# Divisors on four column quarters, and key sums two blocks at a time, in a fused hash attention and gated feed-forward kernel

## The chip, the cores and the metric

The kernel runs on one core of a Trainium2 chip. The core has a matrix engine (TensorE, PE in the profile), a vector engine (VectorE, DVE), a scalar engine (ScalarE, ACT), a general engine (GpSimd, POOL) and queues that issue transfers (SyncE, SP, has the one that matters here). Each works through its own instructions in order and waits on semaphores for the others. SBUF is the memory the engines work in, 128 partitions wide; PSUM holds what TensorE writes. The metric is the device time of one execution in microseconds (us).

## The reference

Two blocks, one after the other. Attention has 4 batches of 8 heads, 768 tokens, head dimension 64. Queries and keys are projected on 6 random directions, the signs of the projections make a bucket number, and a query sees only the keys of its own bucket:

```python
mask = q_bucket[:, :, :, None] == k_bucket[:, :, None, :]
scores = np.where(mask, scale * np.matmul(q, k.transpose(0, 1, 3, 2)), -1000000000.0)
attn = np.exp(scores - np.max(scores, axis=-1, keepdims=True))
attn = attn / (np.sum(attn, axis=-1, keepdims=True) + 1e-09)
attn_out = np.matmul(attn, v)
```

The result, laid out as x with 3072 rows (tokens) and 512 columns, goes through a feed-forward with 2048 inner columns; the result is float32:

```python
h = x @ w_in
sp = np.maximum(h, 0.0) + np.log1p(np.exp(-np.abs(h)))
out = (h * erf(sp)) @ w_out
```

## The kernel before

**Pairs, halves and groups.** The 32 heads are worked in 16 pairs, two heads (`ab` = 0, 1) side by side in the two halves of the partitions. The 768 queries of a pair are two halves of 384 (HS), so there are 32 halves `h` (NH). The 768 keys of a half are six blocks of 128, in two groups `n` of three (GC). A score (`score`, L521) puts 128 keys on the partitions and 384 queries of both heads on the columns: for each head a bfloat16 product of the bucket bits, which adds a penalty for a foreign bucket, and a float32 product of k and q, into one PSUM tile `st`, of which there are three. ScalarE takes the exponential of it into SBUF (`exponential`, L535): block e, 128 keys by 2 x 384 queries, with one more column of ones. There are nine blocks of e, used in a ring.

**Sums and products of e.** The divisor of the softmax is the sum of e over all 768 keys. VectorE first adds the six blocks of a half into one, five additions of 128x768 (`sum_keys`, L547). TensorE then adds over the partitions by a product with ones (`divisor`, L592): per head one product with 64 columns of ones, the heads on partitions 0 to 63 and 64 to 127 of `z_ps`, so each sum stands there 64 times. Meanwhile TensorE has formed e times v (`weigh`, L561, tile `av`), two heads on the two column halves of the array. ScalarE copies both out (`keep_divisor` L604 to `z`, `leave` L613 to `x`).

**The reciprocals go through DRAM.** For a pair, SP stores one row of z for each head (`spread`, L633), loads the 1536 sums back as 128 partitions by 12 (`gather`, L637), VectorE adds a small number and takes the reciprocal (`invert`, L645 and L648), SP stores them (`ungather`, L653) and loads each head's row into 64 partitions (`widen`, L662). VectorE multiplies x by them (`normalise`, L670), and SP stores the pair's x (`send`, L676). In the same SP queue stand the loads of later pairs (`start_pair`, L342 and L347).

**Beside it.** For each next pair TensorE projects q and k (`hash_bits`, L358), ScalarE takes the signs, VectorE spreads them (L382, L392). ScalarE squares q and k into x_sum, a tile that the feed-forward uses later, only to sum the squares (`measure`, L579). 32 pieces of w_in and w_out, which arrive in float64, are converted by ScalarE and VectorE (L445 to L507), and VectorE forms sums of w_in (`presum_weights`, L691) and of the first block of x (`presum_x`, L326). A last part, `late`, does the divisor of the last half and the last pair's chain at the start of the feed-forward.

**The order of the work** is fixed by a planner, `arrange`. Every step is an `op` with an engine, a cost in us, a rank, the steps that it must follow, and a delay until others may see it; the planner lets each engine take the open step that can start first, lowest rank first. TensorE's own order is written out: for half h the scores of groups 2h+1 and 2h+2, the bits of the next pair after every second half, the divisor of half h-1, then both groups of `weigh` of half h. Its costs there are 0.82 us for a score, 2.02 for a group of `weigh`, 0.72 for a divisor. Tiles are followed for semaphores by the parts of them that are read and written.

**The feed-forward** (from about 340 us) forms both products with seven block products instead of eight, on the sums made before; TensorE, VectorE and ScalarE work through it in 24 steps. The change does not touch it.

Of the kernel before, what the change touches and what calls it, by code (L numbers as in the profile page):

```python
# [54 lines left out]
F32 = mybir.dt.float32  # L55
BF16 = mybir.dt.bfloat16
# [3 lines left out]
ALU = mybir.AluOpType  # L60
# [3 lines left out]
P = 128  # L64
# [16 lines left out]
class Op:  # L81
# [20 lines left out]
    exponential=(3.56, 5.29),  # L102
# [91 lines left out]
def kernel(  # L194
# [11 lines left out]
    nc = tc.nc  # L206
    B, H, S, D = v.shape
    NBIT = proj2.shape[1] // 2
    NPAIR = B * H // 2
# [3 lines left out]
    HS = S // 2  # L213
    JP = NPAIR // B
    GC = NC // 2
# [18 lines left out]
    ones = const.tile([P, D], F32, name="ones")  # L234
# [7 lines left out]
    blocks = []  # L242
# [16 lines left out]
    for c, (end, factor) in enumerate(  # L259
# [9 lines left out]
            out=steps[:, c : c + 1],  # L269
            in0=row,  # L270
# [12 lines left out]
    def bank(name):  # L283
        return misc.tile([P, 512], F32, name=name, tag="bank")
# [116 lines left out]
    def attention():  # L401
        NS = NPAIR * 4
        with (
# [17 lines left out]
            raws = {}  # L421

            def fetch_weights(n):
                if n >= len(pieces):
# [102 lines left out]
                        )  # L527

            def block(n, c):
                return etiles[(n * GC + c) % len(etiles)]  # L530

            def exponential(n, c):
                st = pairs[n // 4].pop(("st", n, c))
# [2 lines left out]
                    out=e[:, :, 0:HS], in_=st[:, :, 0:HS], func=AF.Exp, scale=scale  # L536
                )

            def sum_keys(n, c):
                d = pairs[n // 4]  # L540
                key = "sum", n // 2 % 2
                if n % 2 == 0 and c == 1:
                    d[key] = sums.tile([P, 2, HS], F32, name="sum", tag="sum")
                    before = block(n, 0)[:, :, 0:HS]
                else:
                    before = d[key]
                nc.vector.tensor_tensor(  # L547
                    out=d[key], in0=before, in1=block(n, c)[:, :, 0:HS], op=ALU.add
                )

            def weigh(n):
                half, g = n // 2 % 2, n % 2
# [23 lines left out]
            def measure(i, n, half):  # L576

                cols = slice(half * HS, (half + 1) * HS)
                nc.scalar.activation(  # L579
                    out=x_sum[:, 0, :, :].rearrange("p k t -> p (k t)")[:, 0:HS],  # L580
                    in_=pairs[i]["qk"[n]][:, cols],
                    func=AF.Square,
                    accum_out=stats[:, n, i, half : half + 1],
                )

            def divisor(h):

                i, half = divmod(h, 2)
                d = pairs[i]
                z = d["z_ps"] = bank("z_ps")[:, 0:HS]  # L590
                for ab in range(2):
                    nc.tensor.matmul(  # L592
                        out=z[ab * D : ab * D + D, :],
                        lhsT=ones,
                        rhs=d["sum", half][:, ab, :],
                        start=True,
                        stop=True,
                    )
# [28 lines left out]
            def spread(i):  # L627

                d = pairs[i]
                zd = d["zd"] = dram.tile([2, S], F32, name="zd", tag="zd")  # L630
                d["zc"] = small.tile([P, 2 * S // P], F32, name="zc", tag="zc")
                for ab in range(2):
                    nc.sync.dma_start(out=zd[ab : ab + 1, :], in_=d["z"][ab * D : ab * D + 1, :])  # L633

            def gather(i):
                d = pairs[i]
                nc.sync.dma_start(  # L637
                    out=d["zc"],
                    in_=d.pop("zd")[:, :].rearrange("a (p c) -> (a p) c", c=2 * S // P),
                )  # L640

            def invert(i):
# [6 lines left out]

            def ungather(i):  # L650
                d = pairs[i]
                rd = d["rd"] = dram.tile([2, S], F32, name="rd", tag="rd")
                nc.sync.dma_start(  # L653
                    out=rd[:, :].rearrange("a (p c) -> (a p) c", c=2 * S // P), in_=d["zc"]
                )
# [88 lines left out]
            for what, n in order:  # L744
                if what == "score":
                    i = n // 4
                    after = tuple(("weigh_bits", i, ab) for ab in range(2)) + (("copy_bits", i),)
                    for c in range(GC):
                        free = (slots[-3],) if len(slots) >= 3 else ()
                        pe(score, (n, c), 0.82, after + free)  # L750
                        slots.append(("exponential", n, c))
                elif what == "bits":
                    pe(bits_of, (n,), 1.34, (("start_pair", n), slots[-3]))
                    slots.append(("sign_of", n))
                elif what == "divisor":
                    last = 2 * n + 1
                    pe(divisor, (n,), 0.72, (("sum_keys", last, GC - 1), ("keep_divisor", n - 1)))
                else:
                    h = n // 2
                    after = (("exponential", n, GC - 1),)  # L760
                    if n % 2 == 0:
                        after += (("leave", h - 1), ("leave_plain", (h - 1) // 2))
                    pe(weigh, (n,), 2.02, after)
            for n in range(NS):
                for c in range(GC):
                    op(
                        exponential,
                        (n, c),
                        "ACT",
                        0.735,  # L770
                        (0, n, c),
                        (
                            ("score", n, c),
                            ("weigh", n - 3),
                            ("sum_keys", n - 3, c),
                            ("sum_keys", n - 3, max(c, 1)),
                        ),
                    )
                    if n % 2 or c:
                        after = (("exponential", n, c), ("exponential", n, 0))  # L780
                        after += (("sum_keys", n, c - 1), ("sum_keys", n - 1, GC - 1))
                        if n % 2 == 0:
                            after += (("divisor", n // 2 - 2),)
                        op(sum_keys, (n, c), "DVE", 0.92, (1, n, c), after)
            for h in range(NH - 1):
                i = h // 2
                op(
                    keep_divisor,
                    (h,),
                    "ACT",  # L790
                    0.48,
                    (0, 2 * h, -1),
                    (("divisor", h), ("send", i - 1) if i == NPAIR - 1 else ("widen", i - 1)),
                )
# [5 lines left out]
            for i in range(NPAIR):  # L800
# [32 lines left out]
                        )  # L833
                if i == NPAIR - 1:
                    continue
                op(spread, (i,), "SP", 0.8, (0, n, 0), (("keep_divisor", 2 * i + 1),), late=3.0)
# [788 lines left out]
```

## Time and profile before

| | |
|---|---|
| median of 13 runs | 937.61 us (935.67 to 939.91) |
| the profiled execution | 935.43 us, its span 933.5 us |
| TensorE busy | 918.1 us, 98% |
| VectorE busy | 835.0 us, 89% |
| ScalarE busy | 775.6 us, 83% |
| TensorE's granted clock, mean | 0.999 |
| five groups in attention: st, e, sum, av, z_ps | L521, L535, L547, L561, L592 |

How to read it: the page first gives each engine's busy time and its share of the span, then the span in 40 slices with the busy tenths of each engine. The chain of work that ended last is followed back from the last instruction, at each step to what released it; its shares say which engine set the end, and its pieces in order of time show what followed what. A group is a line, an engine and a shape, with the number of instructions, the busy time, the mean time of one in ns, and the idle time before it. `st<-q,k 64*128` is a product into st whose stationary part has 64 rows and 128 columns of the array. A float32 product is recorded as two passes.

### The profile page before, as it was taken

The numbers are of one execution on the slowest core, as the hardware profiler recorded it, in microseconds if no ns is written. First come the engines' busy times: TensorE is split into PE (matmuls) and PEld (weight loads), VectorE is DVE, ScalarE is ACT, GpSimd is POOL, SyncE is SP. The second block draws the span as 40 slices with busy tenths as digits, with TensorE's granted clock in tenths as the row PEclk, the third lists the DMA queues.
The fourth block names the chain that finished last, engine by engine and source line by source line (L and its number), as shares of the span: only waits on it lengthen the run. The fifth ranks groups of instructions, "written<-read, shape, count | busy, mean of one in ns | idle before, by whom it ended". The sixth has DMA issues, their size and how long they took to land.

```text
span 933.5 us, 12887 instructions
## 1 busy us (share of the span) xinstructions
PE 918.1 (98%) x4875; PEld 666.2 (71%) x4875; DVE 835.0 (89%) x1099; ACT 775.6 (83%) x1002; POOL 17.4 (2%) x35
## 2 busy tenths in 40 slices
PE   8999999999999999999999999999999999999997
PEld 3444444444444458888888888888888888888885
DVE  5999998999999977899999889998899788988995
ACT  6887788767887848999998998899989997899892
POOL 0000000000000000000000000000000000000000
PEclk9999999999999999999999999999999999999999
DMA  8455555565655223010222112201221111111211
GB/s 198 119 132 153 132 148 140 144 197 150 160 153 139 90 90 109 1 46 35 78 69 80 34 39 75 80 34 34 79 62 52 34 56 57 34 34 37 77 35 48
DMA packets 59222, 80.91 MB, mean 87 GB/s; under 512 B 33264, under 2 KB 41968, under 8 KB 59152
## 3 DMA queue, kind: packets, MB, share of 16 engines
q1 hardware_dynamic: 54496, 64.08, 24.0%
q0 software_dynamic: 4352, 15.73, 5.5%
q8 instruction: 40, 0.66, 0.3%
q14 instruction: 30, 0.25, 0.1%
q10 hardware_dynamic: 304, 0.20, 0.1%
HBM read 64.07 MB, written 15.93 MB: 86 GB/s over the span
## 4 chain that ended last, share of the span: by engine, by line
PE 90%; DVE 5%; DMA 2%; ACT 1%; issue 1%; SPq 1%; DVEq 0%; ACTq 0%
PE M L1184 30%; PE X L1044 27%; PE st L521 14%; PE av L561 11%; PE M L1044 3%; PE z_ps L592 2%; PE bits L358 2%; DVE sum L547 2%; DMA zc<-zd 1%; DMA zd<-z 1%; PE warm L698 0%; DVE e L1098 0%; DVE top L481 0%; DVE w_sum L691 0%; DVE h L1126 0%
## 5 line engine op out<-in xcount | busy, mean ns | idle before, releaser
L1111 DVE SCALAR_TENSOR_TENSOR e<-w,e 128x1024 f32<-128x1024 f32 x144 | 173.4, 1220 | 6.2 <-ACT w L1107 3.0
L1107 ACT ACTIVATE w<-w,cq 128x1024 f32<-128x1024 f32 x144 | 160.6, 1143 | 1.9
L535 ACT ACTIVATE e<-st 128x768 f32<-128x768 f32 x192 | 149.1, 816 | 12.0 <-PE st L521 11.8
L521 PE MATMUL st<-q,k 64*128 64x384 f32 x768 | 155.4, 482 | 0.0
L1184 PE MATMUL M<-w_out_sb,h 128*128 128x256 f32 x576 | 140.3, 379 | 0.4 <-DVE h L1126 0.4
L547 DVE TENSOR_TENSOR sum<-sum,e 128x768 f32<-128x768 f32 x128 | 122.2, 954 | 8.2 <-ACT e L535 0.3
L561 PE MATMUL av<-e,v 128*64 128x385 f32 (+1 forms) x768 | 129.4, 486 | 0.0
L1044 PE MATMUL X<-x,w_in_sb 128*128 128x256 f32 x512 | 121.1, 379 | 0.0
L1184 PEld LDWEIGHTS M<-w_out_sb,h 128*128 128x128 f32 x576 | 109.2, 190 | 16.0 <-DVE h L1126 1.3
L1044 PEld LDWEIGHTS X<-x,w_in_sb 128*128 128x128 f32 x512 | 97.0, 190 | 13.8 <-ACT h L1062 0.6
L561 PEld LDWEIGHTS av<-e,v 128*64 128x64 f32 x768 | 55.2, 137 | 68.8 <-issue 68.1
L1184 PE MATMUL M<-wt,S 128*128 128x256 f32 x384 | 93.4, 379 | 0.4 <-DVE S L1141 0.4
L521 PEld LDWEIGHTS st<-q,k 64*128 64x128 f32 x768 | 68.5, 188 | 33.9 <-issue 33.6
L1044 PE MATMUL X<-x_sum,w_sum 128*128 128x256 f32 x344 | 81.7, 380 | 1.8 <-ACT h L1062 1.8
L1184 PEld LDWEIGHTS M<-wt,S 128*128 128x128 f32 x384 | 72.9, 190 | 10.7 <-DVE S L1141 0.8
L1044 PEld LDWEIGHTS X<-x_sum,w_sum 128*128 128x128 f32 x344 | 65.0, 190 | 12.0 <-ACT h L1062 3.3
L1062 ACT COPY h<-X 128x512 f32<-128x512 f32 x85 | 49.0, 576 | 22.3 <-PE X L1044 21.4
L521 PE MATMUL st<-qb,kb 64*128 64x384 bf16 x384 | 63.9, 324 | 3.5 <-ACT e L535 2.4
L1088 DVE SCALAR_TENSOR_TENSOR w<-w,e 128x1024 f32<-128x1024 f32 x48 | 58.4, 1221 | 9.7 <-ACT w L1083 9.6
L1126 DVE TENSOR_TENSOR h<-h,e 128x1024 f32<-128x1024 f32 x48 | 58.0, 1220 | 6.1 <-ACT e L1122 5.9
L1102 ACT ACTIVATE w<-e 128x1024 f32<-128x1024 f32 x48 | 50.4, 1050 | 13.4 <-DVE e L1098 13.1
L1098 DVE TENSOR_TENSOR e<-e,w 128x1024 f32<-128x1024 f32 x48 | 57.4, 1218 | 2.6 <-ACT e L1094 2.6
(107 smaller groups left out, 1337.6 us busy)
## 6 DMA issues: line engine op xcount, KB each, us to landing
wt<-wt SPq DMA_DIRECT2D x24, 768.0 KB
raw<-in_w_out_dram POOLq DMA_DIRECT2D x16, 512.0 KB, 3.9
raw<-in_w_in_dram POOLq DMA_DIRECT2D x14, 512.0 KB, 4.1
v<-in_v_dram SPq DMA_DIRECT2D x32, 192.0 KB
xs<-x SPq DMA_DIRECT2D x16, 384.0 KB
q<-in_qkT_dram SPq DMA_DIRECT2D x30, 192.0 KB
k<-in_qkT_dram SPq DMA_DIRECT2D x30, 192.0 KB
r<-rd SPq DMA_DIRECT2D x30, 192.0 KB
```

Source lines behind the costliest of these rows:

```text
L521: nc.tensor.matmul(out=st[:, ab, 0:HS], lhsT=d["k" + src][rows, keys], rhs=d["q" + src][rows, cols], start=(part == 0), stop=(part == 1),)
L535: nc.scalar.activation(out=e[:, :, 0:HS], in_=st[:, :, 0:HS], func=AF.Exp, scale=scale)
L547: nc.vector.tensor_tensor(out=d[key], in0=before, in1=block(n, c)[:, :, 0:HS], op=ALU.add)
L561: nc.tensor.matmul(out=d["av"][rows, 0:w], lhsT=d["v"][:, g * GC + c, rows], rhs=e[:, ab, 0:w], start=(g == 0 and c == 0), stop=(g == 1 an ...
L1044: nc.tensor.matmul(out=d[where][:, u, :], lhsT=a[:, kc, f : f + P], rhs=b[:, kc, :], start=(first and u == 0 and kc == 0), stop=(last and ...
L1088: nc.vector.scalar_tensor_tensor(out=w, in0=w, scalar=-1.0, in1=st[p]["e", v], op0=ALU.add, op1=ALU.subtract)
L1098: nc.vector.tensor_tensor(out=s, in0=s, in1=st[p].pop(("w", v)), op=ALU.subtract)
L1102: nc.scalar.activation(out=z, in_=st[p]["s", v], func=AF.Square)
L1107: nc.scalar.activation(out=q, in_=z, func=AF.Square, bias=cq[:, j : j + 1])
L1111: nc.vector.scalar_tensor_tensor(out=s, in0=st[p].pop(("q", v, j)), scalar=ERF_Q[j][1], in1=s, op0=ALU.add, op1=ALU.mult,)
L1126: nc.vector.tensor_tensor(out=h, in0=h, in1=st[p].pop(("s", v)), op=ALU.mult)
L1184: nc.tensor.matmul(out=banks[name][:, sub, :], lhsT=a[:, u, sub * P : (sub + 1) * P], rhs=b[:, u, :], start=(c == 0 and k == 0), stop=(c = ...
```

## The change

Four things are changed, all in attention.

The nine blocks of e become one tile, `e_all`, so that two neighbouring blocks can be read as one operand. `sum_keys` becomes a short list of steps for a half (`sum_steps`): the first adds blocks 0 and 1 to blocks 2 and 3 in one operation of 128x1536, the second adds blocks 4 and 5, and the third adds the two parts of the sum. Where the ring wraps inside the half, blocks 0 and 1 are added to 3 and 4, then block 2, block 5 and the two parts one at a time. The last two halves add block by block as before. The wide sums lie in x_sum and in the second x block of the feed-forward; `measure` therefore gets a small tile of its own, and the first `presum_x` waits for the third last divisor.

`divisor` makes four products of 32 columns of ones with 192 columns of the sum each, on the four quarters of the array's columns, instead of two of 64 with 384. A head's 384 sums stand in two quarters of the partitions, 192 columns each. `keep_divisor` copies 192 columns, `spread` stores the four rows of a pair in one transfer, and `gather`, `ungather` and `widen` follow the new order of half, head and query.

The planner's costs follow: 0.42 for a divisor, 1.72 for a wide addition, 0.34 for `keep_divisor`, 0.4 for `spread`.

```diff
-            etiles = [ep.tile([P, 2, HS + 1], F32, name=f"e{n}") for n in range(3 * GC)]
-            for e in etiles:
-                nc.vector.memset(e[:, :, HS : HS + 1], 1.0)
+            junk = ep.tile([P, HS], BF16, name="junk")
+            NE = 3 * GC
+            e_all = ep.tile([P, NE, 2, HS + 1], F32, name="e_all")
+            nc.vector.memset(e_all[:, :, :, HS : HS + 1], 1.0)
...
+            wide_sums = [
+                t.rearrange("p a b c -> p (a b c)")[:, 0 : 4 * HS].rearrange(
+                    "p (n a c) -> p n a c", n=2, a=2
+                )
+                for t in (x_sum[:, :, :, :], blocks[1][:, :, :].rearrange("p k (a t) -> p k a t", a=2))
+            ]
...
             def block(n, c):
-                return etiles[(n * GC + c) % len(etiles)]
+                return e_all[:, (n * GC + c) % NE, :, :]
...
-            def sum_keys(n, c):
-                d = pairs[n // 4]
-                key = "sum", n // 2 % 2
-                if n % 2 == 0 and c == 1:
-                    d[key] = sums.tile([P, 2, HS], F32, name="sum", tag="sum")
-                    before = block(n, 0)[:, :, 0:HS]
-                else:
-                    before = d[key]
-                nc.vector.tensor_tensor(
-                    out=d[key], in0=before, in1=block(n, c)[:, :, 0:HS], op=ALU.add
-                )
+            def sum_steps(h):
+                at = [(2 * h * GC + k) % NE for k in range(2 * GC)]
+                if h >= NH - 2:
+                    return [((0, 1), (0, 1), (1, 1), 0)] + [((k,), "s0", (k, 1), 0) for k in range(2, 6)]
+                if at[3] == at[2] + 1:
+                    return [
+                        ((0, 1, 2, 3), (0, 2), (2, 2), 2),
+                        ((4, 5), "s2", (4, 2), 2),
+                        ((), "s0", "s1", 0),
+                    ]
+                return [
+                    ((0, 1, 3, 4), (0, 2), (3, 2), 2),
+                    ((2,), "s0", (2, 1), 0),
+                    ((5,), "s1", (5, 1), 1),
+                    ((), "s0", "s1", 0),
+                ]
+
+            def sum_keys(h, k):
+                i, half = divmod(h, 2)
+                d = pairs[i]
+                if k == 0:
+                    if h >= NH - 2:
+                        d["sum", half] = sums.tile([P, 1, 2, HS], F32, name="sum", tag="sum")
+                    else:
+                        d["sum", half] = wide_sums[h % 2]
+                s = d["sum", half]
+                _, one, two, where = sum_steps(h)[k]
...
+                into = s[:, 0:2, :, :] if where == 2 else s[:, where : where + 1, :, :]
+                nc.vector.tensor_tensor(out=into, in0=term(one), in1=term(two), op=ALU.add)
...
                 nc.scalar.activation(
-                    out=x_sum[:, 0, :, :].rearrange("p k t -> p (k t)")[:, 0:HS],
+                    out=junk,
                     in_=pairs[i]["qk"[n]][:, cols],
...
             def divisor(h):
                 i, half = divmod(h, 2)
                 d = pairs[i]
-                z = d["z_ps"] = bank("z_ps")[:, 0:HS]
-                for ab in range(2):
+                z = d["z_ps"] = bank("z_ps")[:, 0 : HS // 2]
+                for n in range(4):
+                    ab, part = divmod(n, 2)
                     nc.tensor.matmul(
-                        out=z[ab * D : ab * D + D, :],
-                        lhsT=ones,
-                        rhs=d["sum", half][:, ab, :],
+                        out=z[n * QR : (n + 1) * QR, :],
+                        lhsT=ones[:, 0:QR],
+                        rhs=d["sum", half][:, 0, ab, part * HS // 2 : (part + 1) * HS // 2],
                         start=True,
                         stop=True,
                     )
...
-                nc.scalar.copy(out=d["z"][:, half * HS : (half + 1) * HS], in_=d.pop("z_ps"))
+                nc.scalar.copy(
+                    out=d["z"][:, half * HS // 2 : (half + 1) * HS // 2], in_=d.pop("z_ps")
+                )
...
-                zd = d["zd"] = dram.tile([2, S], F32, name="zd", tag="zd")
+                zd = d["zd"] = dram.tile([2, 4, HS // 2], F32, name="zd", tag="zd")
                 d["zc"] = small.tile([P, 2 * S // P], F32, name="zc", tag="zc")
-                for ab in range(2):
-                    nc.sync.dma_start(out=zd[ab : ab + 1, :], in_=d["z"][ab * D : ab * D + 1, :])
+                nc.sync.dma_start(
+                    out=zd.rearrange("h n c -> n h c"),
+                    in_=d["z"][0 : 3 * QR + 1 : QR, 0:HS].rearrange("n (h c) -> n h c", h=2),
+                )
...
                     nc.sync.dma_start(
-                        out=d["r"][ab * D : ab * D + D, :],
-                        in_=rd[ab : ab + 1, :].broadcast_to([D, S]),
+                        out=d["r"][ab * D : ab * D + D, :].rearrange("p (h c) -> p h c", h=2),
+                        in_=rd[:, ab : ab + 1, :].rearrange("h a c -> a h c").broadcast_to([D, 2, HS]),
                     )
...
-                    last = 2 * n + 1
-                    pe(divisor, (n,), 0.72, (("sum_keys", last, GC - 1), ("keep_divisor", n - 1)))
+                    pe(divisor, (n,), 0.42, (("sum_keys", n, last_sum(n)), ("keep_divisor", n - 1)))
...
-                        op(sum_keys, (n, c), "DVE", 0.92, (1, n, c), after)
...
+                    if k == 0:
+                        after += (("divisor", h - 2),)
+                    op(sum_keys, (h, k), "DVE", 1.72 if where == 2 else 0.92, (1, 2 * h + 1, k), after)
...
-                op(presum_x, (0, k), "DVE", 0.62, (2, 31, 8 + k), (("load_x", 0), ("presum_x", 0, k - 1), ("measure", NPAIR - 1, 1, 1)))
+                op(presum_x, (0, k), "DVE", 0.62, (2, 31, 8 + k), (("load_x", 0), ("presum_x", 0, k - 1), ("divisor", NH - 3)))
```

More of the change, by code (lines that the diff above doesn't have):

```diff
@@ L415, in big @@
                 return psum.tile([P, 2, 512], F32, name=name, tag="big", bufs=3)
-            etiles = [ep.tile([P, 2, HS + 1], F32, name=f"e{n}") for n in range(3 * GC)]
-            for e in etiles:
-                nc.vector.memset(e[:, :, HS : HS + 1], 1.0)
+            junk = ep.tile([P, HS], BF16, name="junk")
+            NE = 3 * GC
+            e_all = ep.tile([P, NE, 2, HS + 1], F32, name="e_all")
+            nc.vector.memset(e_all[:, :, :, HS : HS + 1], 1.0)
             pairs = {}
             raws = {}
+            NH = NPAIR * 2
+            wide_sums = [
[4 more added lines that the diff above has]
+            ]
             def fetch_weights(n):
@@ L537, in exponential, with last_sum, term @@
                 )
-            def sum_keys(n, c):
-                d = pairs[n // 4]
-                key = "sum", n // 2 % 2
-                if n % 2 == 0 and c == 1:
-                    d[key] = sums.tile([P, 2, HS], F32, name="sum", tag="sum")
-                    before = block(n, 0)[:, :, 0:HS]
-                else:
-                    before = d[key]
-                nc.vector.tensor_tensor(
-                    out=d[key], in0=before, in1=block(n, c)[:, :, 0:HS], op=ALU.add
-                )
+            def sum_steps(h):
[14 more added lines that the diff above has]
+                ]
+            def last_sum(h):
+                return len(sum_steps(h)) - 1 if h >= 0 else 0
+            def sum_keys(h, k):
[8 more added lines that the diff above has]
+                _, one, two, where = sum_steps(h)[k]
+                def term(what):
+                    if isinstance(what, str):
+                        n = int(what[1])
+                        return s[:, 0:2, :, :] if n == 2 else s[:, n : n + 1, :, :]
+                    first, count = what
+                    first = (2 * h * GC + first) % NE
+                    return e_all[:, first : first + count, :, 0:HS]
+                into = s[:, 0:2, :, :] if where == 2 else s[:, where : where + 1, :, :]
+                nc.vector.tensor_tensor(out=into, in0=term(one), in1=term(two), op=ALU.add)
             def weigh(n):
@@ L638, in gather @@
                     out=d["zc"],
-                    in_=d.pop("zd")[:, :].rearrange("a (p c) -> (a p) c", c=2 * S // P),
+                    in_=d.pop("zd")
+                    .rearrange("h n c -> (h n c)")
+                    .rearrange("(p c) -> p c", c=2 * S // P),
                 )
@@ L651, in ungather @@
                 d = pairs[i]
-                rd = d["rd"] = dram.tile([2, S], F32, name="rd", tag="rd")
+                rd = d["rd"] = dram.tile([2, 2, HS], F32, name="rd", tag="rd")
                 nc.sync.dma_start(
-                    out=rd[:, :].rearrange("a (p c) -> (a p) c", c=2 * S // P), in_=d["zc"]
+                    out=rd.rearrange("h a c -> (h a c)").rearrange("(p c) -> p c", c=2 * S // P),
+                    in_=d["zc"],
                 )
@@ L763, in attention @@
                     pe(weigh, (n,), 2.02, after)
+            sums_after = {}
+            for h in range(NH):
+                for k, (_, *terms, _) in enumerate(sum_steps(h)):
+                    for term in terms:
+                        if not isinstance(term, str):
+                            for b in range(term[0], sum(term)):
+                                at = (2 * h + b // GC, b % GC)
+                                sums_after[at] = (("sum_keys", h, k),)
             for n in range(NS):
@@ L771, in attention @@
                         (0, n, c),
[L772 to L777, printed above, removed]
-                    )
[L779 to L783, printed above, removed]
-                        op(sum_keys, (n, c), "DVE", 0.92, (1, n, c), after)
+                        (("score", n, c), ("weigh", n - 3)) + sums_after.get((n - 3, c), ()),
+                    )
+            for h in range(NH):
+                for k, (blocks_, _, _, where) in enumerate(sum_steps(h)):
+                    after = tuple(("exponential", 2 * h + b // GC, b % GC) for b in blocks_)
+                    after += (("sum_keys", h, k - 1), ("sum_keys", h - 1, last_sum(h - 1)))
+                    if k == 0:
+                        after += (("divisor", h - 2),)
+                    op(sum_keys, (h, k), "DVE", 1.72 if where == 2 else 0.92, (1, 2 * h + 1, k), after)
             for h in range(NH - 1):
@@ L790, in attention @@
                     "ACT",
-                    0.48,
+                    0.34,
                     (0, 2 * h, -1),
@@ L835, in attention @@
                     continue
-                op(spread, (i,), "SP", 0.8, (0, n, 0), (("keep_divisor", 2 * i + 1),), late=3.0)
+                op(spread, (i,), "SP", 0.4, (0, n, 0), (("keep_divisor", 2 * i + 1),), late=3.0)
                 op(gather, (i,), "SP", 0.35, (0, n, 1), (("spread", i),), late=4.5)
```

## The prediction

> **What bounds the kernel now.** I read the page's engine totals first, then its 40 slices, then the chain that ended last, first as a share of the span and then piece by piece for the attention stage, because every edit lies there.
>
> ```profile
> PE 918.1 (98%) x4875; PEld 666.2 (71%) x4875; DVE 835.0 (89%) x1099; ACT 775.6 (83%) x1002; POOL 17.4 (2%) x35
> ...
> PE   8999999999999999999999999999999999999997
> ...
> DVE  5999998999999977899999889998899788988995
> ...
> PE 90%; DVE 5%; DMA 2%; ACT 1%; issue 1%; SPq 1%; DVEq 0%; ACTq 0%
> ```
>
> TensorE (PE) is busy 98% of the span and carries 90% of the chain. VectorE (DVE) is nearly full in the first fourteen slices, which are attention; this makes it the second bound. The pieces of the chain show one pair of heads in the steady part:
>
> ```profile
> 220.53 4.95 PE st L521 x36
> 225.48 1.44 PE bits L358 x8
> 226.92 0.65 PE z_ps L592 x4
> 227.56 3.88 PE av L561 x24
> 231.44 4.95 PE st L521 x36
> 236.39 0.80 PE z_ps L592 x4
> 237.19 3.87 PE av L561 x24
> 241.06 4.95 PE st L521 x36
> ```
>
> The columns are start, length, work. A pair takes 241.06 - 220.53 = 20.53 us of TensorE alone, nothing between. A float32 product shows as two passes, and two products on the two column halves of the array run together: av is 24 records in 3.87, so 12 rounds of 0.323 us for 384 columns; z_ps after bits is 4 records in 0.65, so 2 rounds of the same. But z_ps after st takes 0.80. The 0.15 more is the change of the array's division, from two row halves (st, shape 64*128) to two column halves (128*64); bits after st pays it too (8 records, 4 rounds of 0.323 = 1.29, shown 1.44). Back into st the timeline gives 0.807 us from score to score, six are 4.84, and st shows 4.95: 0.11 for the return. These switch prices decide the forecast.
>
> From the 21.71 us mark to 313.58 lie 14 pairs, 14 x 20.53 = 287.4 us, in 291.9 us: 4.45 us of stalls, in two places where VectorE also forms sums of w_in (L691). The second reads so:
>
> ```profile
> 185.25 0.94 DVE x L670
> ...
> 186.21 2.27 DMA xs<-x
> ...
> 188.58 0.49 ACT x L613
> ...
> 194.34 0.98 PE st L521 x6
> ```
>
> VectorE normalises a pair late, the store of x lands late, ScalarE waits with the copy out of av, the exponentials queue behind it, and TensorE loses 2.9 us.
>
> **The change, part by part. The divisors on TensorE (the new `divisor`).** Removed per half: two products of 384 columns, 64 wide, 0.65 us. Added: four of 192 columns, 32 wide, eight records. The trace has no four products at once. Its shorter rounds are those of the feed-forward, 8 records of 256 columns in 350.32 to 352.05, 0.216 each; with 0.323 for 384 this is a straight line of 0.84 ns a column, so 192 columns are 0.162. If all four run together, a half costs 2 x 0.162; if only two at a time, as in every row here, 4 x 0.162, which is what it costs now. I take four: going from one product to two on the same 128 partitions cost nothing (av and z_ps rounds fit the same line as the feed-forward's single ones). Gain: 32 halves x 0.324 = 10.4 us; bounds 0 and 10.4.
>
> Against it stand switches. Now z_ps, bits and av have one division; afterwards z_ps alone has quarters. The 14 divisors that follow bits pay a switch in, which they do not now; those and the 17 that follow st pay a switch out to av, which is now free. (The last one lies between feed-forward products, and has both already, its z_ps being 0.80 there too.) That makes 45 new switches. No row shows a switch between halves and quarters of columns, so bounds are 0 and 0.15; I take 0.135, between the 0.15 in and the 0.11 out, because all changes of division seen cost that. 45 x 0.135 = 6.1. Net 4.3 us faster.
>
> The Trainium skill speaks here against the change: "TensorEngine Tiling (Array Packing)", Key Properties, says that changing the tiling mode, not merely the tile, drains the engine. The 0.65 beside 0.80 agrees for rows to columns; by the rule halves to quarters drain as well, and the sum stays at 4.3; without it, it would be 10.4. "TensorE: Matmul & The Clock Gate", Part 3, gives 2.38 times for three column tiles; at that efficiency, 0.79, my estimate is 0.20 instead of 0.16 a round and a net gain of some 1.5 us.
>
> **The sums on VectorE.** Removed per half: five additions of 768 elements, 954 ns (122.2 us for 128). Added: two of 1536 and one of 768, or, where the ring of nine blocks wraps (every third half), one of 1536 and three of 768.
>
> ```profile
> L547 DVE TENSOR_TENSOR sum<-sum,e 128x768 f32<-128x768 f32 x128 | 122.2, 954 | 8.2 <-ACT e L535 0.3
> ...
> L1098 DVE TENSOR_TENSOR e<-e,w 128x1024 f32<-128x1024 f32 x48 | 57.4, 1218 | 2.6 <-ACT e L1094 2.6
> ```
>
> Additions of 512 (L1141, 687 ns), 768 and 1024 lie on a line of 1.04 ns an element, so 1536 is 954 + 798 = 1.75 us. A half falls from 4.77 to 4.45 or 4.61; with the last two halves as before, 30 x 0.27 = 8.0 us of VectorE, and up to 0.06 us of issue for each instruction saved. In the steady part this is hidden, since TensorE sets the pace there. In the two stalled stretches, some 53.6 + 20.6 us or 7 halves, it shortens VectorE's backlog by about 1.9 us, while a faster TensorE asks 7 x 0.13 = 0.9 sooner: 1.0 of the 4.45 goes. Bounds: all 4.45 gone, or as much again added, because a 1.75 us addition stands in front of the mask products (kb, qb), which st waits for, and of the normalisation. The wide addition waits for the fourth exponential of a half; behind it in VectorE's queue stand the weight conversions, which have slack. The divisor that reads it comes at least six scores, 4.8 us, after the sixth exponential, and two more additions need 2.7. A block of e is written again seven or more exponentials later (5.7 us at 816 ns), so ScalarE doesn't wait either.
>
> **The rest.** `keep_divisor` copies 192 columns instead of 384: 473 ns against 576 for 512 elements at L1062, 0.8 ns a column, 0.31 us, 5 us less on ScalarE in all; ScalarE is at 79% in the steady stretch, hidden; nothing lost without that cover. `spread` issues one transfer instead of two, about 0.3 us less on SP ahead of `gather`; its landing (zd<-z 3.1 to 3.35 us in the chain) has 8 pieces of 768 bytes instead of two rows of 3 KB: hidden by TensorE in the steady part, and where it is not, in the two stalled pairs, 0.3 us either way each; I take zero. `widen` has twice the pieces at half the size (1.5 KB): the last wait for it was 3.25 us (below); I take zero, at worst 1 us, which the steady chain hides because r does not appear in it. `measure` writes a small tile in bfloat16, same 524 ns. Nine memsets of 60 ns become one before any data is there: zero.
>
> `presum_x` of the first block now waits for the third last divisor, because the sums live in x_sum. Two of its four additions ran at 324.13 and 324.86; that divisor ends at 328.8. They move into the gap that VectorE has before the feed-forward:
>
> ```profile
> 338.46 0.69 DVE L326 TENSOR_TENSOR x_sum<-x,x_sum 128x512 f32<-128x512 f32 x1
> 342.39 1.02 DVE L670 SCALAR_TENSOR_TENSOR x<-x,ev,r 128x768 f32<-128x768 f32 x1 [3.25 <-DMA r<-rd]
> ```
>
> 1.4 us fit into 3.25, and the first product that reads them starts at 344.15. Cost zero; if all four land behind the normalisation at 342.39, they end at 343.3 + 2.8 = 346.1, and TensorE loses 2 us.
>
> **Sum.** 4.3 + 1.0 = 5.3 us off the profiled execution's 935.43 (span 933.5, 1.9 around it): 930.1. That execution lies 2.2 below the median of 937.61, so in terms of the median 932.3 us.
>
> **The rivals.** (1) The four quarters do not run together. The trace has only two at once. Then nothing is gained, and 45 x 0.135 = 6.1 us are paid: 943.7 at the median, or 942.7 if VectorE still returns 1.0. It decides from a round of 0.24 us on: 64 x (0.323 - 0.243) + 1.0 is then the 6.1 of the switches. This is the one on the other side. (2) Halves to quarters costs no switch: 10.4 + 1.0 faster, 926.2. For it: no row shows it; against it: both other changes of division cost 0.11 to 0.15. (3) The new order of VectorE makes stalls. Attention is at 94.5% of VectorE in the long steady stretch (107.36 of 113.59 us), and the chain pair by pair (normalise, store, fetch, divisors out and back) runs through one SP queue, and its stores are issued at 144.35, 165.15 and 186.21, that is every 20.8 to 21.1 us there, no faster than TensorE. As much stall again as now, 4.45, leaves 4.3 - 4.45, about 937.8; two of the 2.9 us kind beyond that, 943.6. (4) The wide additions give back all stalls: 937.61 - 4.3 - 4.45 = 928.9.
>
> **How the numbers follow.** The forecast with its neighbour (4) has 0.52, own range 928 to 935.5; rival 1 has 0.17, rival 2 0.09, rival 3 0.22. 0.2%, 1.9 us, is about what a measurement of this kernel can tell from no change. Faster: 0.46 of the first, all of rival 2, 0.03 of rival 3: 0.58. Within: 0.04 of the first, 0.07 of rival 3, 0.01 of rival 1: 0.12. Slower: 0.02 + 0.12 + 0.16 = 0.30. The range runs from 927.5 to 943.0: it leaves out most of rival 2 below, and above the worse half of rivals 1 and 3.
>
> **What would show it.** Right: z_ps x8 in about 0.48 us of chain after st or bits, av beginning 0.13 late, a pair at 20.53 - 0.19 - 0.04 = 20.30; sum rows of 1.75 us; the stalls at about 3.5. Wrong: z_ps at 0.65 or more plus a switch (rival 1); av directly behind z_ps (rival 2); new pieces of DVE or DMA in the chain between 20 and 340 us (rival 3); a first feed-forward product waiting for L326.

## The result, and the profile after

The changed kernel takes 933.2 us (median of 11 runs, 930.45 to 934.42), the kernel before 937.09 us (49 runs, 934.83 to 939.91). The ratio is 0.995, with a 95% interval of 0.9941 to 0.996: 0.5% faster, or 4.7 us (the two medians themselves lie 3.9 us apart). The forecast was 932.3 us, and the range 927.5 to 943.0. One execution of a run below, e2, took 2259.44 us; it counts in e2's median of 934.38 us and not in its ratio, and the median of the other six is 933.78.

The engine totals and the chain's shares of the changed kernel look as before; the edit is too small to show there:

```profile
PE 915.6 (98%) x5003; PEld 661.0 (71%) x5003; DVE 829.5 (89%) x1041; ACT 771.9 (83%) x1002; POOL 17.7 (2%) x35
...
PE 90%; DVE 5%; DMA 2%; issue 1%; ACT 1%; DVEq 0%; ACTq 0%
```

It shows in the pieces of the chain (start, length, work), here one pair of heads in the steady part:

```profile
228.43 4.95 PE st L529 x36
233.38 0.46 PE z_ps L635 x8
233.85 4.02 PE av L602 x24
237.87 4.95 PE st L529 x36
242.82 1.44 PE bits L358 x8
244.26 0.46 PE z_ps L635 x8
244.72 4.03 PE av L602 x24
248.76 4.95 PE st L529 x36
```

z_ps takes 0.46 us wherever it stands, instead of 0.80 after st and 0.65 after bits. av, which took 3.87 or 3.88, takes 4.02 or 4.03. The pair takes 20.33 us instead of 20.53. The groups of the sums (busy us, mean ns, then idle time before) give the price of a wide addition, 1752 ns:

```profile
L590 DVE TENSOR_TENSOR x_sum<-e_all 128x1536 f32<-128x1536 f32 x15 | 26.3, 1752 | 3.8 <-ACT e_all L543 3.8
L590 DVE TENSOR_TENSOR x_sum<-x_sum 128x768 f32<-128x768 f32 x15 | 14.3, 954 | 0.2
```

Stalls remain. The chain of the changed kernel shows the pattern that the prediction read in the second stall, at a new place: VectorE normalises a pair (L721), its store lands late, ScalarE's copy out of av waits, exponentials queue behind it, and then TensorE goes on:

```profile
286.89 1.02 DVE x L721
287.93 4.20 DMA xs<-x
...
292.60 0.83 ACT e_all L543
...
293.47 2.60 PE st L529 x18
```

To compare kernels I took from each trace the times at which av of each half starts. "Pair" below is the time for two halves where nothing stalls, and "stalls" is what the first 29 intervals between those starts (14 pairs and a half) hold beyond that. Both come from one profiled execution of each kernel. Before: pair 20.52, stalls 4.6 us. After: 20.32 and 3.5.

The two profiled executions differ by 2.2 us of span (933.5 and 931.3), less than the medians, and the difference lies at the start. The first av begins at 17.66 us in the profile of before and at 19.41 in that of after, and TensorE's early rounds stayed slow for longer there (the second projection's passes are recorded at 0.90 us instead of 0.54). From the first av to the first feed-forward product it is 322.93 us (17.66 to 340.59) against 318.51 (19.41 to 337.92): 4.4 us less, of which 15 x 0.21 = 3.1 are the pairs, 1.1 the stalls and 0.2 the last half. The rest of the span is 592.9 and 593.4 us.

### The profile page after: what moved, and what is told of

Read it like the earlier page. It is cut to its first block, busy times and chain, and to the rows that moved or that the text cites. A ratio compares the mean times of both kernels' runs of the same rounds, so it can differ in the third digit from the quotient of the medians.

```text
span 931.3 us, 12993 instructions
## 1 busy us (share of the span) xinstructions
PE 915.6 (98%) x5003; PEld 661.0 (71%) x5003; DVE 829.5 (89%) x1041; ACT 771.9 (83%) x1002; POOL 17.7 (2%) x35
## 4 chain that ended last, share of the span: by engine, by line
PE 90%; DVE 5%; DMA 2%; issue 1%; ACT 1%; DVEq 0%; ACTq 0%
PE M L1238 30%; PE X L1098 27%; PE st L529 14%; PE av L602 11%; PE M L1098 3%; PE bits L358 2%; PE z_ps L635 1%; DVE x L590 1%; DMA xs<-x 1%; DMA zd<-z 1%; DVE x_sum L590 1%; DMA zc<-zd 1%; PE warm L749 0%; DVE e L1152 0%; DVE x L721 0%
## 5 line engine op out<-in xcount | busy, mean ns | idle before, releaser
L543 ACT ACTIVATE e_all<-st 128x768 f32<-128x768 f32 x192 | 149.7, 817 | 13.2 <-PE st L529 13.0
L602 PE MATMUL av<-e_all,v 128*64 128x385 f32 (+1 forms) x768 | 131.1, 490 | 0.0
L602 PEld LDWEIGHTS av<-e_all,v 128*64 128x64 f32 x768 | 52.3, 136 | 67.3 <-issue 66.1
L659 ACT COPY x<-av 128x384 f32<-128x384 f32 x32 | 15.3, 478 | 53.8 <-PE av L602 33.6
```

The source lines that it names most:

```text
L543: nc.scalar.activation(out=e[:, :, 0:HS], in_=st[:, :, 0:HS], func=AF.Exp, scale=scale)
L602: nc.tensor.matmul(out=d["av"][rows, 0:w], lhsT=d["v"][:, g * GC + c, rows], rhs=e[:, ab, 0:w], start=(g == 0 and c == 0), stop=(g == 1 an ...
```

## The experiments

Every time is a median with its ratio to the kernel before, run beside it, and the 95% interval of that ratio.

| run | what | us | ratio (95% interval) | pair | stalls |
|---|---|---|---|---|---|
| changed | the change | 933.2 | 0.995 (0.9941 to 0.996) | 20.32 | 3.5 |
| e1 | divisors only | 942.31 | 1.0054 (1.0042 to 1.0066) | 20.32 | 11.2 |
| e2 | sums only | 934.38 | 0.9961 (0.9943 to 0.9979) | 20.53 | 2.8 |
| e3 | changed, divisor before bits | 931.58 | 0.9938 (0.9925 to 0.995) | 20.16 | 3.6 |
| e4 | changed, bits and av on quarters too | 933.01 | 0.9957 (0.9943 to 0.997) | 19.86 | 8.3 |
| e5 | changed, three buffers for x | 932.35 | 0.9941 (0.9926 to 0.9956) | 20.31 | 0.2 |
| e6 | e4 with three buffers for x | 934.76 | 0.9968 (0.9953 to 0.9982) | 19.86 | 8.6 |
| e7 | e1 with three buffers for x | 943.1 | 1.006 (1.0047 to 1.0073) | 20.32 | 11.1 |
| e8 | before, three buffers for x | 937.21 | 1.0003 (0.9994 to 1.0013) | 20.52 | 4.1 |
| e9 | e1 with the planner's costs of before | 934.71 | 0.9969 (0.9956 to 0.9983) | 20.31 | 4.6 |
| e10 | e1 with two buffers for keep | 942.48 | 1.0052 (1.0033 to 1.0071) | 20.31 | 9.7 |
| e11 | e4 with two buffers for keep | 933.1 | 0.9948 (0.9932 to 0.9965) | 19.86 | 8.8 |
| e12 | e3 with three buffers for x | 930.46 | 0.9933 (0.9918 to 0.9949) | 20.16 | 5.1 |

### The two parts alone

e1 is the kernel before with the new `divisor`, `keep_divisor`, `spread`, `gather`, `ungather` and `widen` and their three costs; the sums stay as they were.

```diff
-                for ab in range(2):
+                for n in range(4):
+                    ab, part = divmod(n, 2)
...
-                        rhs=d["sum", half][:, ab, :],
+                        rhs=d["sum", half][:, ab, part * HS // 2 : (part + 1) * HS // 2],
...
-                    pe(divisor, (n,), 0.72, (("sum_keys", last, GC - 1), ("keep_divisor", n - 1)))
+                    pe(divisor, (n,), 0.42, (("sum_keys", last, GC - 1), ("keep_divisor", n - 1)))
```

> Only the divisors' part of the change: four products on column quarters, one transfer for a pair's divisors; the sums of e stay as before, one block at a time. Theory (TensorE gains 0.19 us a half after st and 0.04 after bits, the sums give back about 1 us of stalls): z_ps in 0.46 us of the chain and av in 4.02, a pair of 20.31 us instead of 20.53, stalls in attention as before or up to 1 us more, in all 3.0 to 4.3 us faster than before. Rival (the relief of VectorE is what made the changed kernel faster): less than 1.5 us faster.

Measured: 942.31 us, slower than before by 0.54%. TensorE got what was expected, a pair of 20.32 us, but the stalls went from 4.6 to 11.2 us. Neither theory had that.

e2 is the changed kernel with those six functions and their costs put back:

```diff
-                for n in range(4):
-                    ab, part = divmod(n, 2)
+                for ab in range(2):
...
-                        rhs=d["sum", half][:, 0, ab, part * HS // 2 : (part + 1) * HS // 2],
+                        rhs=d["sum", half][:, 0, ab, :],
...
-                    pe(divisor, (n,), 0.42, (("sum_keys", n, last_sum(n)), ("keep_divisor", n - 1)))
+                    pe(divisor, (n,), 0.72, (("sum_keys", n, last_sum(n)), ("keep_divisor", n - 1)))
```

> Only the sums' part of the change: wide additions, their places in x_sum and the x block, and the later presum of x; the divisors on two column halves and two transfers as before. Theory: z_ps 0.65 after bits and 0.80 after st, a pair of 20.53 us, stalls 4.45 us or less; 0 to 1.5 us faster than before. Rival (the sums carry the gain): 3 to 5 us faster than before with the stalls nearly gone.

Measured: 934.38 us. TensorE's pair is as before, 20.53, and the stalls are 2.8 us, 1.8 less. The ratio says 2 to 5 us, so the sums alone are worth more than the theory's 0 to 1.5 us, though its rival's "stalls nearly gone" did not come either. The profiled execution, one of the slower ones of e2 (935.88 us), shows less: from the first av to the first feed-forward product 321.31 us, 1.6 less than before. The parts do not add up: by the ratios e1 lost 5.1 us, e2 won 3.7, and together they win 4.7.

### Why the divisors alone were slower

The waits of e1 (us in all, times, longest) name ScalarE's preparation of a weight piece, `keep` (L445), which may overwrite its one buffer only when VectorE has masked the piece before (L481). In ScalarE's queue exponentials stand behind it:

```profile
ACT keep L445 <- DVE top L481: 12.9, 11, 2.3
PE st L521 <- ACT e L535: 9.3, 8, 1.8
```

and its chain shows the sequence:

```profile
244.61 0.70 DVE top L481
...
245.34 0.67 ACT keep L445
246.00 0.71 ACT e L535
...
246.75 1.79 PE st L521 x12
```

That was either VectorE with too much work for a shorter pair, or one tight buffer, or the order in which the planner, with its new costs, had placed these steps. First I gave x a third buffer, since its store was the wait in the stalls of before and after. The room comes from writing the last product of a weight conversion in place:

```diff
-                return xst.tile([P, S], F32, name=what, tag="x" if what == "x" else "z")
+                return xst.tile([P, S], F32, name=what, tag="x" if what == "x" else "z", bufs=3 if what == "x" else 2)
...
-                rest = cvt.tile([P, WP], F32, name="rest", tag="rest")
+                rest = unit[:, :].bitcast(F32)
```

e7, e8 and e5 put it into e1, into the kernel before and into the changed kernel.

> Only the divisors' part of the change (sums as before), with three buffers for x. Theory (ring of x): the 11.2 us of stalls that made this part alone slower than before fall under 3 us, and it is 3 to 5 us faster than the kernel before: 932 to 934. Rival (five additions a half are too much for VectorE at a pair of 20.3 us): stalls of 7 us or more stay, 938 or more.

> The kernel before with three buffers for x and nothing else. Theory (ring of x): its 4.6 us of stalls fall under 1 us, 933 to 934 us. Rival (VectorE): no difference from the kernel before, 937.

> The changed kernel with three buffers for a pair's x instead of two; the room comes from writing the last product of a weight conversion in place instead of into a tile of its own, which moves no work. Theory (the stalls come from the ring of x: the copy out of av for a pair waits until the pair two before it is stored, and that pair's chain over DRAM takes longer than two pairs): the waits of that copy for the store of x are gone, the stalls of 3.5 us fall under 1 us, 2.5 to 3.5 us less than the changed kernel, about 930.3 us. Rival (VectorE has too much work for a pair, so the stalls return at another wait): no difference, 933.

e7: 943.1 us, stalls 11.1. e8: 937.21, stalls 4.1. In both the ring of x was not the main cause. e5: the stalls in the steady part did go, from 3.5 to 0.2 us, but the time only to 932.35, and the intervals of e5 and the changed kernel overlap. Its chain shows where 1.7 us of it went (the last av begins 8.71 us after the one before, instead of 7.02): it waits for a small VectorE step on the previous av (`ev`), which VectorE reaches late.

```profile
330.90 0.43 DVE unit L497
331.33 0.08 DVE ev L665
...
331.45 4.11 PE av L602 x24
```

Then two runs on e1 itself. e10 gives `keep` two buffers (room as before); e9 leaves every tile alone and only gives the planner the old costs, so that the engines' order is that of the kernel before.

```diff
-                keep = cvt.tile([P, WP], I32, name="keep", tag="keep")
+                keep = cvt.tile([P, WP], I32, name="keep", tag="keep", bufs=2)
```

> Only the divisors' part of the change, with the planner's new costs, but two buffers for keep, the tile in which ScalarE prepares a weight conversion and which it can overwrite only when VectorE has masked the piece before (room as before: the last product in place). Theory (ScalarE's square of a weight piece waits there for VectorE, with exponentials queued behind it): these waits, 12.8 us in 11 places with one buffer, go, stalls fall from 11.2 to under 5 us, 933 to 936. Rival (VectorE's backlog returns at another wait): stalls of 8 us or more, 939 or more.

```diff
-                    pe(divisor, (n,), 0.42, (("sum_keys", last, GC - 1), ("keep_divisor", n - 1)))
+                    pe(divisor, (n,), 0.72, (("sum_keys", last, GC - 1), ("keep_divisor", n - 1)))
...
-                    0.34,
+                    0.48,
...
-                op(spread, (i,), "SP", 0.4, (0, n, 0), (("keep_divisor", 2 * i + 1),), late=3.0)
+                op(spread, (i,), "SP", 0.8, (0, n, 0), (("keep_divisor", 2 * i + 1),), late=3.0)
```

> Only the divisors' part of the change, as in the run of that part alone, but the planner is given the costs of before (0.72 for a divisor, 0.48 for its copy, 0.8 for the store), so every engine but for the divisors' own instructions has the order of the kernel before. Theory (the planner's new costs wrote an order in which ScalarE stands earlier at waits for VectorE, and this made that part alone slower, not VectorE's work): stalls of 3 to 6 us instead of 11.2, pair 20.32 us, 932.5 to 935.5. Rival (five additions a half are too much work for VectorE at a pair of 20.3 us, whatever the order): stalls of 9 us or more, 939 or more.

e10: 942.48 us. The waits at `keep` are gone, and others are in their place:

```profile
ACT x L618 <- DMA xs<-x: 18.4, 4, 6.0
PE st L521 <- ACT e L535: 4.0, 4, 1.9
```

In e7, with the third buffer for x, the waits at `keep` stayed as they were in e1 (12.8 us, 11 times); e1's list has no wait for xs. So taking away the wait at `keep` brought out another, and the time stayed. Both buffers in one kernel were not tried on e1. e9: 934.71 us with stalls of 4.6, as in the kernel before, though every instruction of e1 is in it. Up to 336 us ScalarE's and VectorE's instructions stand in the trace of e9 in the order of the kernel before, and in that of e1 in another:

```profile
ACT keep L445 <- DVE top L481: 5.2, 5, 2.0
...
PE st L521 <- ACT e L535: 2.4, 2, 1.2
```

So 942.31 - 934.71 = 7.6 us of e1 are the order that three changed numbers in the planner produced. VectorE's five additions a half fit into a pair of 20.31 us when the order suits. Which of the three numbers does it was not tried.

### What a change of division costs, and four products at once

e3 only swaps two steps in TensorE's order, so that bits and av stand side by side in one division of the array:

```diff
-                if h % 2 == 0 and h // 2 + 1 < NPAIR:
-                    order.append(("bits", h // 2 + 1))
                 if h >= 1:
                     order.append(("divisor", h - 1))
+                if h % 2 == 0 and h // 2 + 1 < NPAIR:
+                    order.append(("bits", h // 2 + 1))
```

> The changed kernel with one edit: in the iterations that have both, the divisor stands before the bits in TensorE's order, so the order is st, z_ps, bits, av. Theory (each change of the array's division costs about 0.145 us, whichever divisions are meant): bits and av follow each other in one division, 14 switches go, 14 x 0.145 = 2.0 us less than the changed kernel, about 931.2 us; av after bits 3.88 us again. Rival (the 0.15 us belongs to the quarter products themselves, such as their eight weight loads): no difference from the changed kernel.

Measured: 931.58 us; its interval overlaps with that of the changed kernel, so the trace must decide. The chain shows the switch go where it was expected: av after z_ps 4.03, av after bits 3.88, the pair 0.16 us shorter.

```profile
254.41 0.46 PE z_ps L635 x8
254.87 4.03 PE av L602 x24
258.90 4.95 PE st L529 x36
263.85 0.46 PE z_ps L635 x8
264.31 1.44 PE bits L358 x8
265.75 3.88 PE av L602 x24
```

e4 puts bits and av on quarters as well:

```diff
-                    for ab in range(2):
-                        rows = slice(ab * D, ab * D + D)
+                    for quarter in range(4):
+                        rows = slice(quarter * QR, quarter * QR + QR)
...
-                            rhs=e[:, ab, 0:w],
+                            rhs=e[:, quarter // 2, 0:w],
```

> The changed kernel with bits and av also on column quarters: four products of 32 columns where there were two of 64, the same sums in the same places. Theory: the four run together in the same 0.323 us a round, and z_ps, bits and av have one division, so all 45 new switches go: z_ps 0.33 after bits and 0.46 after st, av 3.88, 45 x 0.145 = 6.5 us less than the changed kernel, about 926.7 us, if VectorE and the transfers keep up. Rival (TensorE cannot issue twice as many products and weight loads): av longer than 4.02 us; at the 0.067 us a record that st takes on average it would be 6.4 us, 32 x 2.4 = 77 us slower.

Measured: 933.01 us, the changed kernel's time. On TensorE the theory held: twice as many products, 48 records instead of 24, take the same 3.87 us, z_ps behind bits takes 0.33, two rounds without a switch, and the pair is 19.86 us, 0.46 shorter.

```profile
212.51 0.46 PE z_ps L636 x8
212.97 3.87 PE av L603 x48
216.84 4.95 PE st L530 x36
...
242.53 1.43 PE bits L359 x16
243.96 0.33 PE z_ps L636 x8
```

15 x 0.46 = 6.9 us were won there, and 8.3 - 3.5 = 4.8 lost again in stalls. Of the 2.1 us left, 0.8 went before the last av (7.80 us after the one before, instead of 7.02), and the medians show no gain. Giving e4 a third x buffer (e6) or a second keep buffer (e11), with the edits shown above, changed nothing that can be told:

> bits, z_ps and av all on column quarters, with three buffers for x. Theory (ring of x): the 8.3 us of stalls that this order of TensorE had with two buffers fall under 2 us, and the pair of 19.86 us shows: 6 to 8 us less than with two buffers, 925 to 927 us. Rival (VectorE, some 19.5 us of work and gaps a pair, is now the bound): the pairs stay at 20.3 us or more and the time at 931 or more.

> bits, z_ps and av on column quarters with the wide sums, and two buffers for keep. Theory (the square behind which exponentials queue): stalls fall from 8.3 to about 4 us and the time to about 928.5. Rival (VectorE sets 20.6 us a pair): 931 to 934, stalls of 7 us or more at other waits.

e6: 934.76 us, stalls 8.6; e11: 933.1, stalls 8.8. From the av of half 7 to that of half 27 a pair took 20.6 us in e4 and 20.7 in e6, so TensorE no longer sets the pace there. In e6 the waits sit at `keep` and at the mask products:

```profile
ACT keep L454 <- DVE top L490: 12.5, 11, 2.3
...
PEld L530 <- DVE kb L383: 7.3, 7, 1.6
```

Whether VectorE's amount of work or again its order sets those 20.6 us is open: the order of e4 was not planned anew.

The last run puts e3 and the third buffer for x together.

> The changed kernel with the divisor before the bits and three buffers for x, the two edits that helped it one at a time. Theory (they act on different things, the switches and the waits for the store of x): pair 20.16 us as with the first, stalls under 1.5 us as with the second, 929 to 930.5 us, 0.75 to 0.9% below the kernel before. Rival (the stalls of the first had other causes, the divisors' way through DRAM): stalls of 3 us or more and 931.5 or more.

Measured: 930.46 us, the lowest median, though its interval touches those of e3 and of the changed kernel. The pair is the 20.16 us of e3. The waits for the store of x are gone, but there are 5.1 us of stalls, where TensorE waits for VectorE's late mask products. So the theory was right about the time and the rival about the stalls. The trace has only 0.7 us less than that of the changed kernel between the first av and the feed-forward (317.84 us against 318.51), so the lower median is not explained:

```profile
PEld L529 <- DVE kb L382: 5.1, 4, 2.1
PE st L529 <- DVE kb L382: 2.7, 3, 1.5
```

## Why the prediction was right, point by point

**The divisors on TensorE.** Forecast: z_ps about 0.48 us of the chain, av 0.13 later, a pair of 20.30, 4.3 us in all. Measured: 0.46, 0.15, 20.32. e9, which has this part with the old order, is 2.9 us faster by its ratio (1.6 to 4.1), and its pairs give 15 x 0.21 = 3.1. The four quarters do run together (rival 1 falls: eight records in 0.46 us less a switch are two rounds of 0.16). Halves to quarters is a change of division like the others (rival 2 falls): 0.14 us in, since z_ps after bits is 0.46 instead of 2 x 0.16, and 0.15 out; e3 removed one a pair and won 0.16, e4 removed three and won 0.46. The Trainium skill's rule in "TensorEngine Tiling (Array Packing)", Key Properties, that changing the tiling mode drains the engine, agrees with this cost for 64 to 32 columns; that the time is a drain, no run here shows. The estimate of 0.20 us a round, worked out from the 2.38 times in the Trainium skill's "TensorE: Matmul & The Clock Gate", Part 3, was too slow: the two rounds of z_ps behind bits in e4 take 0.33.

**The sums on VectorE.** 1.75 us for 1536 elements was forecast, 1.752 measured. VectorE's additions in attention fell from 152.3 to 143.6 us, 8.7 where 8.0 was forecast.

The step "1.0 of the 4.45 goes" came out at 1.1 (4.6 to 3.5), but its working does not hold, and that the number fits is in part luck. The prediction let VectorE's saved time and TensorE's sooner demand, 1.9 and 0.9 us, make the difference. The first fits in size: with the old costs the wide sums take 1.8 us of stalls (e2, one profiled execution as everywhere). The second does not: the faster TensorE in the old order adds none (e9, 4.6). And the prediction put the planner's new costs at nothing, without a reason. With the old sums they add 6.6 us of stalls (11.2 in e1, 4.6 in e9). With the wide sums beside them the stalls are 3.5, only 0.7 more than in e2. So a term larger than the whole gain that was forecast, 5.3 us, was left out, and beside the wide sums nearly all of it happened not to show. The prediction named a new order as rival 3, but looked for its cause in VectorE's load and in the transfers' loop, and sized it by the stalls that the profile of before happened to show.

The reading of the second stall was also incomplete. The prediction names the late store of x. In the chain of before, between the copy out of av at 188.58 and the score at 194.34, stands a wait at `keep`, the one that e1 has so often:

```profile
191.33 0.96 DVE sum L547
192.29 0.61 DVE top L481
...
192.92 0.67 ACT keep L445
193.59 0.71 ACT e L535
```

e8 took the waits for the store away, and this interval between two avs fell from 12.56 us only to 11.73, where 9.63 is that without a stall.

**The rest.** The first presum of x ran whole, at 337.20 to 339.81 us, behind the attention's last sums, and the first product that reads it started at 341.47: no cost, as forecast. keep_divisor's copy took 312 ns (0.31 forecast). No wait for r showed in the changed kernel's steady part.

**Rival 3 and rival 4.** New stalls did come (at 152 and 296 us, 1.4 and 1.7 us), and old ones went; the balance is 1.1 us better.

What stays open: why the new costs give a worse order. A divisor of 0.42 us is less than the 0.46 us and the 0.15 us of switch that it takes, which would place ScalarE's and VectorE's steps too early; no run tested that. Nor is it known why the wide sums suffer so little from the new costs, whether by VectorE's smaller load or by the other order that they bring: the changed kernel with the old costs was not run.

## What to carry to other kernels

Where a written order or a planner sets the queues, a changed cost figure is a change of its own: three numbers made 7.6 us here, more than the edit that they belonged to. Apply the edit once with the old figures before judging it. Products with few output columns can share the array, but count the changes of division beside the rounds saved, and put the products that share a division next to each other. When a stall's wait is removed and the time stays, as in e6, e7, e10 and e11, ask which engine was late, and whether by its load or by its place in the order.

## What was unexpected of the hardware

Four 32-column float32 products on the four column quarters, 48 records in a row in e4, kept the full rate: 3.87 us, the same as 24 records on halves. And the start differs between the profiled executions, and not by kernel (e7 starts early, and e1, from which it differs by its buffers alone, late): the first av began at 17.7 us in two of the profiled executions (before, e7) and at 19.1 to 20.1 in the other twelve, with the early passes at 0.9 us instead of 0.5, though the granted clock reads 1.00 in all of them through the first 14 us. That makes up to 2.4 us between these executions, and it hid part of the gain in the two profiles.
